# Two ordering keys in a hand-planned attention and MLP kernel: the ranks of the flags behind a far-V product, the far V of tile 3 behind a mask of tile 2

## The chip, the cores and the metric

The kernel runs on one core of a Trainium2 chip. The metric is the device time of one execution in microseconds (us); lower is better. A core has five engines that run their own instruction streams in order and meet at semaphores: TensorE (PE, matmuls), VectorE (DVE), ScalarE (ACT), GpSimd (POOL) and SyncE (SP, which here only issues DMAs). In the profile PEld is the loading of TensorE's weights.

## What is computed

Attention over 4 batches, 8 heads, 768 positions and head size 64, followed by a two-layer MLP over the 3072 tokens that come out of it:

```python
scores = scale * np.matmul(q, k.transpose(0, 1, 3, 2))
stream_keep = causal & (is_sink | in_win)          # 4 sink positions, a window of 64
mask = np.where(retr, causal, stream_keep)         # one flag for each head: full or streaming
a = softmax(np.where(mask, scores, -1e9)); attn_out = np.matmul(a, v)
x = attn_out.transpose(0, 2, 1, 3).reshape(B * S, H * D)
h = x @ w_in                                        # 512 -> 2048
g = h - np.tanh(h)
return g @ w_out                                    # 2048 -> 512
```

The flags (`is_retrieval`) are data: the kernel learns only on the chip which heads are full and which are streaming. Inputs and output are float32; the kernel's matmuls are float16.

## The kernel before, in words

**Tiles.** The 3072 tokens are 12 tiles of 256 (`TT`), three tiles to a batch (`NG`), so tiles 0 to 2 are batch 0 and tiles 3 to 5 batch 1. A tile has four pairs of heads; pair number n is 4 t + hp, so tile 2 has pairs 8 to 11. For each pair the kernel transposes q and k (`st_T`, or DMA transposes, `turn`), multiplies them (`st_S`, PE L1063, with the exponential on ACT at L1076), masks the block at the diagonal on DVE (`mask`: L1117 in tile 2, L1127 and L1092 from tile 3 on), multiplies by V (`st_A`, PE L1156) and divides by the sums (DVE L1176, L1188 or L1203). Tiles 0 and 1 have their mask added by a matmul (L1052) instead.

**The MLP of a tile.** `H_unit` makes 256 columns of the hidden layer: eight matmuls (PE L1267) into a PSUM bank, a tanh on ACT (`th`, L1279), and one DVE instruction `gt` (L1286) that reads the bank and the tanh, forms h - tanh(h) and lets the bank go. `O_group` multiplies by `w_out` (PE L1325); ACT copies the result out (`ot`, L1299) and SP stores it (L1311).

**Far V.** For a key block that lies before the window, a streaming head may see the sinks alone. So the kernel keeps V twice: `v1` as it is, and `vf`, the far V, where the rows that a streaming head must not see are zero. In batch 0 GpSimd makes `vf` by `scale_v` (L725), one product for each of the key blocks 0 to 3: blocks 0 and 1 come with tile 0, blocks 2 and 3 with tile 1. From batch 1 on, heads are sorted by their flag, and `vf` is made by `spread` (L690 products, L699 and L710 copies, all on GpSimd).

**Ranks of the flags.** `by_rank` (L834) sorts the heads: 15 small DVE instructions (L841 to L908), four mask builders `m4r` (L917) and two copies for `mS`; then GpSimd and DVE each read the ranks into registers (L939). `gather` for tile 3 and later (GpSimd L636 and L672) picks heads by these registers out of the raw loads (`rawqk`, `rawv`, L592). Tile 3's raw loads are issued from GpSimd's queue, behind the register read for all but the first of them; those of later tiles from SP.

**Tile 4's gate.** A small GpSimd instruction pair `hold` (L576, L580) writes into tile 4's raw buffers once the last part of `w_out` has landed; so SP can't issue the loads of tile 4 before it.

**What sets the order.** All work is first listed by `Plan.op(engine, estimated ns, function, r=keys read, w=keys written)`. An entry depends on the last writer of each key that it reads. `Plan.run` then plays the list through with its estimates: whenever an engine comes free, it takes, of the entries whose dependencies are done, the one with the lowest number (number in the list, unless `prio` is given). It also hands out the PSUM banks and models that a DVE entry with `port=True` waits for a GpSimd entry that holds the port. What comes out is one fixed order for each engine; the functions are then called in that order. A key is known to the planner alone. The waits that the chip obeys come from the tiles that instructions really share, so a key that names data which an instruction doesn't touch moves the instruction in its engine's order and adds no wait on the chip.

**The two places.** `LATE` is a list of keys that each of the 15 small instructions of `by_rank` reads besides its own; before, it is `("x16", 3)`, which is written by the DVE instruction that divides the last pair of tile 0. `spread(3)` lists two L690 products, the L699 copy and the L710 copy; before, they read only `v1` and the flags.

Of the kernel before, what the change touches and what calls it, by code (L numbers as in the profile page):

```python
# [16 lines left out]
class Plan:  # L17
# [28 lines left out]
    def op(self, eng, ns, fn, r=(), w=(), dma=None, prio=None, port=False):  # L46
        i = len(self.ops)
        deps = set()
        for k in r:
            if k in self.writer:  # L50
                deps.add(self.writer[k])
            if k[0] in self.PSUM:
                deps.update(j for j in self.readers.get(k, ()) if self.ops[j][0] != eng)
            self.readers.setdefault(k, []).append(i)
        for k in w:
            if k in self.writer:
                deps.add(self.writer[k])
            elif k[0] in self.BANKS:
                self.first[i] = self.first.get(i, ()) + (k,)
            deps.update(self.readers.get(k, ()))  # L60
            self.writer[k] = i
            self.readers[k] = []
        for key in (*r, *w):
            if isinstance(key, tuple) and key[0] in self.BANKS:
                self.held.setdefault(key, set()).add(i)
            elif isinstance(key, tuple) and key[0] in self.bufs:
                self.users.setdefault(key[:2], []).append(i)
        deps.discard(i)
        self.ops.append((eng, ns, fn, deps, dma, i if prio is None else prio, port))
        return i  # L70
# [185 lines left out]
def kernel(  # L256
# [17 lines left out]
    HP = H // 2  # L274
# [5 lines left out]
    NG = S // TT  # L280
# [6 lines left out]
    fast = n_sink_i <= 64 and window_i <= 64  # L287
# [3 lines left out]
    def pool(name, bufs=1, **kw):  # L291
# [30 lines left out]
    rflagr = const.tile([128, NGEN], FP32, name="rflagr")  # L322
    rflagr0 = const.tile([128, NGEN], FP32, name="rflagr0")
    thrr = const.tile([128, NGEN], FP32, name="thrr")
    mS = const.tile([128, 5, 128], FP16, name="mS")
# [13 lines left out]
        pt=([128, 2, 512 * NG], FP16), ptn=([128, 2, 512], FP16),  # L339
        x16=([128, NB, 2, D], FP16), x16t=([128, NB, H, D], FP16), rinv=([128, NB, 2], FP32),  # L340
# [13 lines left out]
    GATE = {3: (1, 0), 4: (1, 1)}  # L354
    CUT1 = (-10.5,-6.0,2.25,13.5)
    FLEX = 2
    LEAD = 3
    QUART = 7
    LD = 22
    GA = 8  # L360
    FROM = 3
    BR = 1
    FRONT = "A40"
    LATE = [("x16", 3)]
    BEHIND = [("x16", 1)]
    MASKS = 2
    A2 = (4, 9)
# [2 lines left out]
    def program(first):  # L370
# [43 lines left out]
        def dma(ring, ns, fn, packets, each, r=(), w=(), paced=False, lag=(1100, 1500)):  # L414
            r = list(r) + [FRONT] * (ring == "POOL")
            op(ring, ns, fn, r=r, w=w, dma=(packets, each, paced) + lag)
# [265 lines left out]
        def spread(t):  # L682

            b, g = divmod(t, NG)
            lo = g * NB
            for jb in range(lo, min(lo + NB, 4)):
                fl = rflagr0 if jb == 0 else rflagr
                op(
                    "POOL", 600,
                    lambda jb=jb, fl=fl: nc.gpsimd.tensor_mul(  # L690
                        out=vfs[b]()[:, jb, 0:NGEN, :], in0=v1s[b]()[:, jb, 0:NGEN, :],
                        in1=fl[:].unsqueeze(2).to_broadcast([128, NGEN, D + 1]),
                    ),
                    r=[("v1", b, jb, 0), "rflagr0", "rflagr"], w=[("vf", b, jb, 0)],
                )
            if g == 0:
                op(
                    "POOL", 1060,
                    lambda: nc.gpsimd.tensor_copy(  # L699
                        out=vfs[b]()[0:64, :, NGEN:H, :],  # L700
                        in_=v1s[b]()[0:64, 0, NGEN:H, :].unsqueeze(1).to_broadcast(
                            [64, 4, H - NGEN, D + 1]
                        ),
                    ),
                    r=[("v1", b, 0, 1)], w=[("vf", b, "low")],
                )
            j0, j1 = max(lo, 1), min(lo + NB, 5)
            op(
                "POOL", 60 + 260 * (j1 - j0),
                lambda: nc.gpsimd.tensor_copy(  # L710
                    out=vfs[b]()[64:128, j0 - 1 : j1 - 1, NGEN:H, :],
                    in_=v1s[b]()[64:128, j0:j1, NGEN:H, :],
                ),
                r=[("v1", b, jb, 1) for jb in range(j0, j1)],
                w=[("vf", b, "up", jb) for jb in range(j0, j1)],
            )

# [116 lines left out]
        def by_rank():  # L834

            def dve(ns, fn, r, w):
                op("DVE", ns, fn, r=r + LATE, w=w, port=True)

# [75 lines left out]
            for h in range(NGEN):  # L914
# [6 lines left out]
                    r=["thrr", "A4", "A40", "A41", "A43"], w=["m4r"], port=True,  # L921
# [7 lines left out]
                r=["A4", "A40", "A41", "A43"], w=["mS"], port=True,  # L929
# [1 line left out]
            op(  # L931
                "DVE", 180,
                lambda: nc.vector.tensor_copy(out=mS[:, 4, :], in_=mS[:, 2, :]),
                r=["mS3"], w=["mS"], port=True,
            )
            for e, et in (("POOL", Engine.Pool), ("DVE", Engine.DVE)):

# [64 lines left out]
        pts = {}  # L1002

        def is_near(n):
            return ranked(n // HP) and n % 2
# [336 lines left out]
        def visits(t):  # L1342
            g = t % NG
            gen = [t * HP + hp for hp in range(HP) if not is_near(t * HP + hp)]
            near = [t * HP + hp for hp in range(HP) if is_near(t * HP + hp)]
            if near:
                a, c = gen
                d, e = near
                return {
                    0: [[(a, 0), (d, 0)], [(c, 0), (e, 0)]],  # L1350
                    1: [[(a, 0), (a, 1)], [(d, 0), (c, 0)], [(c, 1), (e, 0)]],
                    2: [[(a, 0), (a, 1)], [(a, 2), (d, 0)], [(c, 0), (c, 1)], [(c, 2), (e, 0)]],
                }[g]
            if g == 0:
                return [[(n, 0)] for n in gen]
            units = [(n, gi) for n in gen for gi in range(g + 1)]
            return [units[i : i + 2] for i in range(0, len(units), 2)]
# [96 lines left out]
        def att_pairs(t):  # L1454

            seq = []
            g = t % NG
            for hp in range(HP):
                n = t * HP + hp
                seq.append(lambda n=n: st_T(n, TE))  # L1460
                units = [(n, gi) for gi in range(g + 1)]
                for i in range(0, len(units), 2):
                    seq.append(lambda u=units[i : i + 2]: st_S(u))
                if hp:
                    seq += [lambda n=n - 1, j=j: st_A(n, j) for j in range(NB)]
                    if not by_dma(t):
                        seq.append(lambda n=n - 1: st_X(n))
            n = t * HP + HP - 1
            seq += [lambda n=n, j=j: st_A(n, j) for j in range(NB)]
            if by_dma(t):  # L1470
                seq.append(lambda: st_X_tile(t))
            else:
                seq.append(lambda n=n: st_X(n))
            return seq
# [32 lines left out]
        def spread_over(fs, lo, hi):  # L1507
            for i, f in enumerate(fs):
                plan.setdefault(max(0, int(lo + (hi - lo) * i / max(len(fs), 1))), []).append(f)

        if first and fast:
            spread_over([by_rank], BR, BR)
        spread_over(att_pairs(1) + [lambda: scale_v(1, SV)], 0, 0)
# [3 lines left out]
        def point(h):  # L1517
            t, ts = divmod(h, 2)
            return slot_of[t, 4 * ts + 3] if t >= 2 else max(0, 13 + 2 * h)

        for b in range(FLEX, NTT // NG) if first and fast else ():
            left = {}
# [4 lines left out]
            for i, vis in enumerate(vs):  # L1527
                s = point(6 * b - LEAD + i)
                for t in sorted({n // HP for n, gi in vis}):
# [10 lines left out]
                for t in range(b * NG, b * NG + NG):  # L1540
                    if max(left[n] for n in range(t * HP, t * HP + HP)) == i:
                        fs.append(lambda t=t: st_X_tile(t))
        for t in range(NG, FLEX * NG if first and fast else NTT):
            b, g = divmod(t, NG)
# [11 lines left out]
                spread_over(attention(t), lo, hi)  # L1556

        for s, what in enumerate(slots):
            if first and fast and s == point(2 * NG * FLEX - LEAD - 1):
                P.split = len(P.ops)  # L1560
            fs = plan.get(s, [])
            mid = (len(fs) + 1) // 2
            for i, x in enumerate(what):
                for f in fs[:mid] if i == 0 else ():
                    f()
                if x[0] == "H":
                    H_unit(*x[1:])
                else:
                    t, ts, f0, f1, c0, c1 = x[1:]
                    O_group(t, ts, f0, f1, c0, c1)  # L1570
                for f in fs[mid:] + between.get(s, []) if i == 0 else ():
                    f()
# [59 lines left out]
```

## Time and profile before

| | |
|---|---|
| runs, us | 231.21, 232.74, 232.95 |
| median, us | 232.74 |
| the profiled execution: its own time, us | 233.06 |
| its span (first to last instruction), us | 231.3 |
| mean granted TensorE clock | 0.990 |
| PE busy in the span, us | 221.7 (96%) |
| DVE / ACT / POOL busy, us | 146.7 / 139.9 / 97.5 |

The profiled execution is 0.32 us above the median of the runs shown, and its own time is 1.76 us more than its span. In the views a row of the timeline reads: start, duration, engine, line, operation, output <- input, shape, count, and in brackets the idle time of that engine before it and what ended it. A row with x2 stands for two instructions and the time from the start of the first to the end of the last. A queue's engine (SPq, POOLq) is the sequencer that issues.

### The profile page before, as it was taken

The page shows a single profiled execution, that of the slowest core. Times are in us where ns is not written, and L with a number is a line of the kernel's source. Part 1 is how long each engine was busy: PE and PEld are TensorE (multiplying, and loading weights), DVE is VectorE, ACT ScalarE, POOL GpSimd, SP SyncE. Part 2 cuts the span into 40 slices and gives each one's busy share as a digit, 9 for nine tenths or more (in the row PEclk, how much of TensorE's full clock was granted, in tenths as well). Part 3 has the DMA queues.
Part 4 walks back from the last instruction along what each step waited for, and adds up shares of the span by engine and source line. Part 5 has one row for each costly group of instructions (what it writes and reads, how often), then busy time and mean ns, then how long its engine had stood idle before and what let it go on. Part 6 is the DMA issues. An engine that isn't in the chain of part 4 may idle for free.

```text
span 231.3 us, 6135 instructions
## 1 busy us (share of the span) xinstructions
PE 221.7 (96%) x2328; PEld 158.7 (69%) x2328; DVE 146.7 (63%) x355; ACT 139.9 (60%) x214; POOL 97.5 (42%) x231
## 2 busy tenths in 40 slices
PE   7879999989999999999999999999999999999992
PEld 6446788768887666766776676765957767766652
DVE  5878887893774766755774776466867547534400
ACT  3817837975566858747547756846875867534420
POOL 8998361980281918684363968280000000000000
PEclk9988999999999999999999999999999999999999
DMA  6999999979999999999979999944121211220112
GB/s 171 150 194 206 186 223 217 208 114 204 198 202 233 195 197 233 206 198 209 248 149 252 222 250 185 212 117 114 48 45 48 60 34 45 67 47 28 48 63 80
DMA packets 102964, 35.31 MB, mean 153 GB/s; under 512 B 90642, under 2 KB 100114, under 8 KB 102930
## 3 DMA queue, kind: packets, MB, share of 16 engines
q1 hardware_dynamic: 85632, 27.14, 56.3%
q0 software_dynamic: 17152, 7.60, 25.1%
q8 instruction: 19, 0.31, 0.6%
q14 instruction: 15, 0.12, 0.2%
q10 hardware_dynamic: 146, 0.13, 0.2%
HBM read 27.26 MB, written 6.29 MB: 145 GB/s over the span
## 4 chain that ended last, share of the span: by engine, by line
PE 84%; DVE 6%; DMA 3%; POOL 2%; ACT 2%; issue 1%; POOLq 0%; DVEq 0%
PE banks L1325 36%; PE banks L1267 34%; PE banks L1063 7%; PE banks L1156 6%; DMA t16p<-in_k_dram 3%; DVE gt L1286 2%; DVE pt L1117 2%; ACT pt L1076 1%; DVE prod L846 1%; POOL v L490 1%; PE banks L968 1%; PE banks L1052 1%; ACT th L1279 1%; DVE QK L951 0%; POOL A L736 0%
## 5 line engine op out<-in xcount | busy, mean ns | idle before, releaser
L1267 PE MATMUL banks<-xT,win 128*128 128x256 f16 x768 | 95.0, 273 | 0.7 <-DVE gt L1286 0.5
L1325 PE MATMUL banks<-wout,gt 128*128 128x512 f16 (+1 forms) x464 | 94.5, 343 | 1.1 <-DVE gt L1286 1.1
L1286 DVE SCALAR_TENSOR_TENSOR gt<-th,banks 128x512 f16<-128x512 f32 x96 | 65.1, 682 | 31.5 <-ACT th L1279 30.7
L1267 PEld LDWEIGHTS <-win 128*128 128x128 f16 x768 | 72.8, 98 | 15.5 <-issue 2.1
L1279 ACT ACTIVATE th<-banks 128x512 f32<-128x512 f32 x96 | 57.1, 601 | 40.5 <-PE banks L1267 39.4
L1076 ACT ACTIVATE pt<-banks 128x768 f16<-128x768 f32 (+1 forms) x60 | 52.9, 920 | 17.3 <-PE banks L1063 16.4
L1325 PEld LDWEIGHTS <-gt 128*128 128x128 f16 x464 | 43.0, 98 | 29.3 <-DVE gt L1286 1.3
L636 POOL CAST t<-rawqk 128x256 f16 x72 | 28.6, 443 | 30.6 <-DMA rawqk<-in_k_dram 14.7
L1299 ACT ACTIVATE ot<-banks 128x512 f32<-128x512 f32 (+1 forms) x28 | 15.0, 535 | 22.0 <-PE banks L1325 21.2
L1188 DVE TENSOR_TENSOR x16t<-banks,rinv 128x128 f32 (+1 forms) x80 | 22.9, 288 | 1.8 <-DVE x16t L1188 0.2
L1099 DVE TENSOR_TENSOR ptn<-ptn,mS 128x512 f16<-128x512 f16 x24 | 10.9, 493 | 17.0 <-ACT ptn L1076 17.0
L1063 PE MATMUL banks<-QK 64*128 64x128 f16 (+1 forms) x364 | 21.4, 241 | 0.0
L672 POOL CAST v<-rawv 128x128 f16 x72 | 19.7, 320 | 0.0
L1063 PEld LDWEIGHTS <-QK 64*128 64x128 f16 x364 | 12.7, 95 | 9.9 <-issue 6.8
L1076 ACT ACTIVATE ptn<-banks 128x1024 f16<-128x1024 f32 (+1 forms) x18 | 17.2, 953 | 3.8 <-PE banks L1063 3.7
L1156 PEld LDWEIGHTS <-pt 128*128 128x128 f16 x420 | 16.3, 97 | 3.8 <-ACT pt L1076 0.7
L1156 PE MATMUL banks<-v,pt 128*128 128x65 f16 x220 | 16.6, 193 | 0.3 <-ACT pt L1076 0.2
L1127 DVE TENSOR_TENSOR pt<-pt,m4r 128x1024 f16<-128x1024 f16 (+1 forms) x18 | 12.4, 686 | 5.0 <-ACT pt L1076 5.0
L1176 DVE RECIPROCAL rinv<-banks 128x4 f32<-128x4 f32 x48 | 8.5, 177 | 8.5 <-PE banks L1156 7.7
L1156 PE MATMUL banks<-vf,pt 128*128 128x65 f16 x200 | 13.1, 193 | 0.0
L661 POOL COPY kc<-QK 128x128 f16<-128x128 f16 x12 | 3.5, 290 | 12.0 <-DMA QK<-t 11.9
L1156 PEld LDWEIGHTS <-ptn 128*128 128x128 f16 x132 | 6.4, 97 | 2.2
(79 smaller groups left out, 137.2 us busy)
## 6 DMA issues: line engine op xcount, KB each, us to landing
out_dram<-ot SPq DMA_DIRECT2D x19, 256.0 KB, 2.5
rawqk<-in_q_dram SPq DMA_DIRECT2D x18, 256.0 KB, 3.8
rawqk<-in_k_dram SPq DMA_DIRECT2D x18, 256.0 KB, 4.4
rawv<-in_v_dram SPq DMA_DIRECT2D x16, 256.0 KB, 4.6
win<-in_moe_w_in_dram POOLq DMA_DIRECT2D x4, 512.0 KB, 11.3
wout<-in_moe_w_out_dram POOLq DMA_DIRECT2D x4, 512.0 KB, 13.2
out_dram<-ot SPq DMA_DIRECT2D x9, 128.0 KB, 3.8
v<-in_v_dram POOLq DMA_DIRECT2D x6, 128.0 KB, 6.8
```

Of the source, the lines that this page charges most:

```text
L636: nc.gpsimd.tensor_copy(out=c5()[:, :, :, s_ : s_ + 1, :], in_=r5()[:, :, :, at, :])
L672: nc.gpsimd.tensor_copy(out=v1s[b]()[:, g * NB : g * NB + NB, RANK[s_] : RANK[s_] + 1, 0:D], in_=rv()[:, :, at, :],)
L1063: nc.tensor.matmul(out=sc()[:, hh, o : o + nb * 128], lhsT=lhsT, rhs=QK[p_, hp, q_0 : q_0 + nb * 128], start=not added, stop=not added or ...
L1076: lambda pt=pt, sc=sc, gi=gi, wid=wid: nc.scalar.activation(out=pt()[:, :, 512 * gi : 512 * gi + wid], in_=sc()[:, :, 0:wid], func=AF.Exp, ...
L1127: nc.vector.tensor_mul(out=pv, in0=pv, in1=m)
L1156: nc.tensor.matmul(out=av()[:, i, hh, :], lhsT=pt()[:, hh, co : co + 128], rhs=vv, start=(jb == first_jb), stop=(jb == qb),)
L1188: nc.vector.tensor_mul(out=xt()[:, :, at, :], in0=av()[:, :, hh : hh + 1, 0:D], in1=rinv()[:, :, hh : hh + 1].unsqueeze(3).to_broadcast([1 ...
L1267: nc.tensor.matmul(out=ph()[:, j, :], lhsT=w_in_t[fb // 4][:, cb, f0 : f0 + 128], rhs=xT()[:, :, cb, :], start=(cb == 0), stop=(cb == HP - 1),
L1279: lambda: nc.scalar.activation(out=th()[:], in_=ph()[:], func=AF.Tanh, scale=1.0 / XS),
L1286: lambda: nc.vector.scalar_tensor_tensor(out=gt()[:, u * FU : (u + 1) * FU, :], in0=th()[:], scalar=-XS, in1=ph()[:], op0=ALU.mult, op1=AL ...
L1299: nc.scalar.activation(out=ot()[:, c0:c1], in_=po()[:, c0:c1], func=AF.Copy, scale=1.0 / XS)
L1325: nc.tensor.matmul(out=po()[:, c0:c1], lhsT=gt()[:, f, ts * 128 : ts * 128 + 128], rhs=w_out_t[:, f, c0:c1], start=(f == 0), stop=(f == NF ...
```

## The change

It adds some parameters that are off (`TRI = ()`, `SPLIT = 1 << 30`, `MSL = []`; with these values the code that reads them does what it did before) and turns two keys:

```diff
-    LATE = [("x16", 3)]
+    LATE = [("vf",0,3,0)]
+    AFTER = {3: 2}
+    TRI = ()
+    SPLIT = 1 << 30
+    MSL = []
...
         def spread(t):
             b, g = divmod(t, NG)
             lo = g * NB
+            after = [("pt", pts[AFTER[t] * HP + HP - 1][1], 0)] if t in AFTER else []
...
-                    r=[("v1", b, jb, 0), "rflagr0", "rflagr"], w=[("vf", b, jb, 0)],
+                    r=[("v1", b, jb, 0), "rflagr0", "rflagr"] + after, w=[("vf", b, jb, 0)],
...
-                    r=[("v1", b, 0, 1)], w=[("vf", b, "low")],
+                    r=[("v1", b, 0, 1)] + after, w=[("vf", b, "low")],
...
-                r=[("v1", b, jb, 1) for jb in range(j0, j1)],
+                r=[("v1", b, jb, 1) for jb in range(j0, j1)] + after,
...
-                r=["mS3"], w=["mS"], port=True,
+                r=["mS3"] + MSL, w=["mS"], port=True,
...
-            if first and fast and s == point(2 * NG * FLEX - LEAD - 1):
+            if first and fast and s == min(SPLIT, point(2 * NG * FLEX - LEAD - 1)):
```

`("vf", 0, 3, 0)` is the far V of key block 3 in batch 0: it is written by the last of the four L725 products on GpSimd. `("pt", pts[11][1], 0)` is the exponential of pair 11, the last of tile 2, first group; its last writer in the list is that pair's mask (L1117). So in the planner the small instructions of `by_rank` may not start before the fourth product is done, and the four instructions of `spread(3)` not before the last mask of tile 2 is done. `visits` gets a branch for tiles in `TRI`, which is empty.

More of the change, by code (lines that the diff above doesn't have):

```diff
@@ L1348, in visits @@
                 d, e = near
+                if t in TRI:
+                    return {
+                        0: [[(a, 0), (d, 0), (c, 0)], [(e, 0)]],
+                        1: [[(a, 0), (a, 1), (d, 0)], [(c, 0), (c, 1), (e, 0)]],
+                        2: [[(a, 0), (a, 1), (a, 2)], [(d, 0), (c, 0), (c, 1)], [(c, 2), (e, 0)]],
+                    }[g]
                 return {
```

## The prediction

> **What bounds the kernel now.** I read the table of stages first (busy time of each engine in windows of the span), to see where PE, the engine with 96% of the span, is not busy; columns are the window, its length, then PE, PEld, DVE, ACT and POOL busy.
>
> ```profile
> 20.00:25.00 5.00, 4.46 (x59) 3.00 (x58) 4.97 (x21) 3.62 (x6) 2.85 (x4) 1.00 1.31 202
> ...
> 50.00:55.00 5.00, 4.02 (x56) 3.33 (x57) 2.90 (x8) 3.08 (x5) 1.07 (x4) 1.00 0.85 171
> ...
> 65.00:100.00 35.00, 35.00 (x389) 25.17 (x387) 23.90 (x55) 24.95 (x37) 20.61 (x56) 1.00 1.12 207
> 100.00:150.00 50.00, 50.00 (x500) 34.55 (x498) 30.97 (x69) 31.57 (x48) 30.10 (x83) 1.00 1.05 215
> ```
>
> From 65 to 150 us PE has no idle time. So whatever PE gains ahead of that is passed on, and nothing can be gained there. Ahead of it two holes stand out: 0.54 us in the window from 20 and 0.98 us in the window from 50. Then the chain of work that ended last, for what ends those holes (start, duration, what):
>
> ```profile
> 18.80 2.39 DVE prod L846
> ...
> 21.21 0.22 DVE cnt L851
> 21.43 0.60 DVE gt L1286
> ...
> 22.08 1.47 PE banks L1267 x12
> ...
> 36.10 0.22 PE banks L1325 x2
> ...
> 47.41 2.71 DVE pt L1117 x2
> ...
> 50.33 0.60 DVE gt L1286
> ...
> 50.98 0.83 PE banks L1325 x6
> ```
>
> Both times the path goes through DVE: PE waits for a `gt`, and the `gt` stands in DVE's queue behind one slow instruction: `prod` of the ranks (2.39 us for 64 columns) and a pair of masks of tile 2 (2.71 us). The timelines of DVE and of GpSimd tell why they are slow:
>
> ```profile
> 18.69 2.49 DVE L846 TENSOR_TENSOR prod<-upto,rflag 128x64 f32<-128x64 f32 x1
> ...
> 21.35 0.68 DVE L1286 SCALAR_TENSOR_TENSOR gt<-th,banks 128x512 f16<-128x512 f32 x1
> ...
> 23.31 0.21 DVE L875 TENSOR_TENSOR prod<-pos_b,iota 128x64 f32<-128x64 f32 x1
> 23.45 0.68 DVE L1286 SCALAR_TENSOR_TENSOR gt<-th,banks 128x512 f16<-128x512 f32 x1
> ...
> 36.26 1.29 DVE L1117 SCALAR_TENSOR_TENSOR pt<-m,pt 128x512 f16<-128x512 f16 x2 [0.23 <-ACT pt L1076]
> ...
> 47.33 2.80 DVE L1117 SCALAR_TENSOR_TENSOR pt<-m,pt 128x512 f16<-128x512 f16 x2
> ...
> 50.84 1.38 DVE L1117 SCALAR_TENSOR_TENSOR pt<-m,pt 128x512 f16<-128x512 f16 x2
> 52.51 0.18 DVE L1176 RECIPROCAL rinv<-banks 128x4 f32<-128x4 f32 x1 [0.28 <-PE banks L1156]
> ```
>
> ```profile
> 19.02 2.07 POOL L725 TENSOR_TENSOR vf<-v,rflag 128x520 f16<-128x520 f16 x2
> ...
> 35.62 0.88 POOL L614 DMA_DIRECT2D wout<-in_moe_w_out_dram  x1 [1.70 <-DMA wout<-in_moe_w_out_dram]
> ...
> 46.58 1.19 POOL L690 TENSOR_TENSOR vf<-v,rflagr 128x260 f16<-128x260 f16 x2
> 47.73 1.04 POOL L699 COPY vf<-v 64x1040 f16<-64x1040 f16 x1
> 48.83 0.76 POOL L710 COPY vf<-v 64x260 f16<-64x260 f16 x1
> 49.65 0.53 POOL L576 CAST rawqk<-wout 1x4 f32<-1x4 f16 x1
> ...
> 50.79 0.28 POOL L661 COPY kc<-QK 128x128 f16<-128x128 f16 x1
> 56.20 0.31 POOL L432 MEMSET v<- 128x48 f16 x1 [5.13 <-PE banks L1156]
> 62.11 2.81 POOL L636 CAST t<-rawqk 128x256 f16 x8 [5.60 <-DMA out_dram<-ot]
> ```
>
> A `prod` of the same size takes 0.21 us at 23.31, where GpSimd runs nothing; the one at 18.69 ends (21.18) just after GpSimd's two far-V products (21.09). A pair of masks takes 1.29 us at 36.26 with GpSimd idle, and 2.80 us at 47.33 beside `spread(3)`, which ends at 49.59. The `gt` at 21.35 takes the same 0.68 us as the one at 23.45: it is not slowed itself, it only stands behind.
>
> **Ranks behind the last far-V product.** Nothing is added or removed; the 15 small instructions move later in DVE's order, and since they touch no `vf`, no wait comes with it. What now stands ahead of them is every DVE entry that is ready before the fourth product's end at 21.09. Two tanhs are ready by then:
>
> ```profile
> 19.25 0.60 ACT L1279 ACTIVATE th<-banks 128x512 f32<-128x512 f32 x1 [0.30 <-PE banks L1267]
> 20.12 0.60 ACT L1279 ACTIVATE th<-banks 128x512 f32<-128x512 f32 x1 [0.28 <-PE banks L1267]
> ...
> 48.76 1.94 ACT L1076 ACTIVATE pt<-banks 128x1024 f16<-128x1024 f32 x2 [0.57 <-PE banks L1063]
> ```
>
> Their `gt`s can run from 19.85 and 20.72 on, instead of at 21.35 and 23.45. PE's hole ahead of 22.08 is 0.54 us (4.46 of 5.00 busy) and closes: the first `gt` would end at about 20.55, before the hole begins at 21.54. The ranks then start at about 21.4, after the products, and their `prod` should cost some 0.2 us: saved DVE time 2.49 - 0.21 = 2.28 us, of which only the 0.54 us lies on the path. Is the gain kept? The nearest limit is the landing of a `w_out` part: GpSimd's issue at 35.62 waited for it, and the chain has PE's `w_out` products at 36.10. If that is the part that they read, PE can gain no more than 36.10 - 35.62 = 0.48 us there. Bounds 0 and 0.54; I take 0.5, nearest to both rows. `cnt` was done at 21.43 before, and will be at about 21.8, with two `gt`s fewer (2 x 0.6 us) behind it; so the ranks come no later, nor do GpSimd's register read and the loads of tile 3 behind it.
>
> **Far V of tile 3 behind the last mask of tile 2.** Again an order alone, now on GpSimd. Behind the four instructions (1.19 + 1.04 + 0.76 = 2.99 us) stood, in this order, the `hold` pair, the `kc` copies up to 50.79, the memset at 56.20 and `gather(4)` at 62.11. The first two groups now go ahead of them: the `hold`, and with it SP's first loads of tile 4, by up to 49.65 - 46.58 = 3.07 us. `kc` can't go before its DMA transposes have landed, and those are not shown to be later than 50.79; so I put the moved block at about 50.8 to 53.8. The memset and `gather(4)` have 5.13 and 5.60 us of waiting ahead of them, which covers it; without that cover tile 4 would be late by up to 2.99 us. The products' results are first read by tile 4.
>
> Gain: the mask pair at 47.33 falls back towards 1.29 us, 1.51 less than 2.80. The `gt` behind it moves from 50.25 to about 48.8, and PE's stop ahead of 50.98 goes: the PE rows below put that stop at 1.06 us (from 49.92), so the change is worth that there and no more. What is late next: the last mask of tile 2. It waits for the second of the two exponentials at 48.76 (end 50.70, with the first part's gain about 50.2), so it runs at 50.2 to 51.5 and its second half meets the moved block. PE has room for that, as its rows at 53.11 and 55.30 show:
>
> ```profile
> 22.08 1.47 PE L1267 MATMUL banks<-xT,win 128*128 128x256 f16 x12 [0.54 <-DVE gt L1286]
> ...
> 50.98 0.83 PE L1325 MATMUL banks<-wout,gt 128*128 128x256 f16 x6 [1.06 <-DVE gt L1286]
> ...
> 53.11 2.36 PE L1325 MATMUL banks<-wout,gt 128*128 128x256 f16 x20
> 55.30 0.25 PE L1156 MATMUL banks<-vf,pt 128*128 128x65 f16 x3
> ```
>
> The product with V of pair 11 at 55.30 waits for this mask, which was done at 52.22: 3.1 us of room, 1.5 us of it used up if PE is earlier by as much. A mask late by up to 1.5 us therefore costs PE nothing there. But the division of pair 10 (52.51) stands behind the mask on DVE and keeps a PSUM bank. Bounds for this part 0 and 1.06; I take 0.9, near the upper one, since the rows before 50.98 show one stop and the rows after it a lot of `w_out` work.
>
> The row at 47.33 has a pair of masks losing 1.51 us to three kinds of GpSimd instruction. The Trainium skill, SBUF — State Buffer, section Who interferes with whom, says that the port which DVE and GpSimd share is a lock held for one whole instruction, by the one that issues first, while the other blocks. By that rule the moved block takes the port once between the halves of the last mask, nothing of the 1.06 us is given back, and the sum would be 1.56 us, 231.2 us by the median. The trace agrees that one blocks the other, and not with the order: the `prod` that began at 18.69 gave way to two products that began at 19.02.
>
> **Sum.** 0.5 + 0.9 = 1.4 us. The profiled execution's 233.06 would be 231.66; by the median of the runs shown, which lies 0.32 below it, 232.74 - 1.4 = 231.3 us, 0.6% faster. About 1% is what a measurement of this kernel can tell from no change.
>
> **The rivals.**
> - Half of it: one of the two holes is filled by another wait, such as the `w_out` landing at 35.6 or the bank of pair 10. For it: both limits lie within a microsecond of the path. Against it: each touches one part alone. 232.74 - 0.7 = 232.0 us.
> - The change doesn't do what it says: since the keys add no wait on the chip, the moved block may still run beside the masks, if GpSimd, freed from it at 46.58, gets through `hold` and `kc` early. `hold` and `kc` would also meet the mask at 47.33. For it: only the upper end of the transposes' landing is shown. Against it: SP's other transposes and `kc` at 50.79 follow the same order. 232.7 us.
> - Slower: the moved block holds DVE up at the last mask from 50.2 on for its whole 2.99 us. The mask would end at 50.2 + 1.29 + 2.99 = 54.5, and the division of pair 10 behind it, which ran at 52.51 before, would run 2.0 us later than before. If its bank is the next that PE needs, all that follows is late by as much: 232.74 + 2.0 = 234.7 us. It decides once the block holds the mask for over 1.0 us (2.99 - 2.0), from where on the division is later than before. For it: the row at 47.33. Against it: there the pair lost 1.51 us to the same block, half of 2.99, and PE has 2.36 us of `w_out` work that needs no new division.
> - Larger: the reordering also takes out stops that are hidden in rows of busy PE, by another 1 us: 230.3 us. Against it: of all that PE waited for between 15 and 62 us, the view of waits (total, times, longest) has 1.6 us in the two holes and 0.4 us beside them:
>
> ```profile
> PE banks L1325 <- DVE gt L1286: 1.1, 1, 1.1
> PE banks L1267 <- DVE gt L1286: 0.5, 1, 0.5
> PE banks L1238 <- DVE x L1203: 0.4, 1, 0.4
> ```
>
> **How the numbers follow.** Forecast 0.55, half of it 0.15, nothing 0.10, slower 0.10, larger 0.10. The three runs spread from 231.21 to 232.95, 0.75%, so the forecast's own 231.3 can measure from 229.8 (231.21 - 1.4) up; the half and nothing cases reach 233, the slower one 234.7. Low end 229.8, high end 233.7: left out are most of the slower case and a part of the larger. Faster by over 1% (below 230.4): the larger case and about a fifth of the forecast's, 0.20. Slower by over 1% (above 235.1): the slower case where it also delays tile 3, which its 234.7 does not hold, 0.08. Within 1%: 0.72.
>
> **What would show it right or wrong.** Right: the first `prod` at about 0.2 us and behind two `gt`s; the PE stop ahead of the third `H_unit` gone; the mask pair of pair 10 near 1.3 us; L690 of tile 3 behind the `kc` copies, from about 50.8; SP's first load of tile 4 before 50.20; PE's window from 50 near 5.00 busy; the end earlier by the sum of the two holes. Wrong: a `prod` of over 1 us still beside L725; a PE stop at 35.6 for `w_out`; the last mask of tile 2 over 2 us with PE idle behind it; or any PE idle time after 62 us, which would mean that a load, not PE, sets the pace there.

## The result, and the profile after

| | runs | median, us | range, us | ratio to before, 95% interval |
|---|---|---|---|---|
| before | 17 | 232.66 | 231.21 to 233.51 | |
| changed | 17 | 231.17 | 230.20 to 232.07 | 0.9942 [0.9923, 0.9961] |

The changed kernel is 0.6% faster: 232.66 x 0.0058 = 1.35 us, between 0.9 and 1.8 us. Its profiled execution took 231.54 us with a span of 229.8 us, 1.5 us less than the span of before. From the first line of the diff on, line numbers are larger by 4 or 5: the ranks' `prod` is L851, the mask L1122, `gt` L1291, the `spread` products and copies L695, L704 and L715.

Where the time went is read best between the same matmuls in both traces: the stretches begin at the scores of the second pair of tile 1, then of tile 2, of tile 2's last pairs, of tile 3 and of tile 4. Stretches of before (window, length, busy time of PE, PEld, DVE, ACT and POOL, granted clock):

```profile
20.63:34.56 13.93, 13.27 (x169) 10.44 (x168) 12.21 (x42) 8.63 (x13) 7.50 (x9) 1.00 1.58 205
34.56:48.33 13.77, 13.63 (x178) 11.03 (x178) 11.32 (x23) 11.75 (x18) 8.22 (x20) 1.00 1.19 201
48.33:56.07 7.74, 6.68 (x99) 5.41 (x99) 4.57 (x9) 4.32 (x6) 2.62 (x6) 1.00 0.78 159
56.07:73.38 17.31, 17.31 (x183) 14.65 (x182) 11.78 (x28) 10.04 (x18) 7.38 (x22) 1.00 1.08 205
```

The same stretches of the changed kernel:

```profile
21.12:34.42 13.30, 13.14 (x171) 10.50 (x170) 11.65 (x42) 8.58 (x13) 7.12 (x9) 1.00 1.60 204
34.42:48.03 13.61, 13.61 (x177) 11.04 (x176) 11.19 (x24) 11.71 (x18) 6.53 (x17) 1.00 1.25 197
48.03:54.54 6.51, 6.51 (x99) 5.50 (x98) 3.38 (x8) 4.22 (x6) 4.71 (x8) 1.00 0.94 211
54.54:71.85 17.31, 17.31 (x183) 14.66 (x181) 11.79 (x28) 10.05 (x18) 7.42 (x22) 1.00 1.04 207
```

The stretch of the ranks is shorter by 0.63 us, the one of tile 2's masks by 1.23, the one between them by 0.16, and the one from tile 3 to tile 4 by nothing, since PE is busy in all of it. Up to the first of these matmuls the changed kernel *lost* 0.49 us (21.12 against 20.63). Sum: 0.63 + 0.16 + 1.23 - 0.49 = 1.53 us, which is the span's 1.5.

DVE in the changed kernel, at the three places:

```profile
13.65 1.50 DVE L938 COPY mS<-mS 128x128 f16<-128x128 f16 x1
...
20.37 0.69 DVE L1291 SCALAR_TENSOR_TENSOR gt<-th,banks 128x512 f16<-128x512 f32 x1 [0.73 <-ACT th L1284]
21.24 0.69 DVE L1291 SCALAR_TENSOR_TENSOR gt<-th,banks 128x512 f16<-128x512 f32 x1 [0.18 <-ACT th L1284]
...
22.17 0.19 DVE L851 TENSOR_TENSOR prod<-upto,rflag 128x64 f32<-128x64 f32 x1
...
47.04 1.28 DVE L1122 SCALAR_TENSOR_TENSOR pt<-m,pt 128x512 f16<-128x512 f16 x2
...
48.44 0.68 DVE L1291 SCALAR_TENSOR_TENSOR gt<-th,banks 128x512 f16<-128x512 f32 x1
50.44 1.72 DVE L1122 SCALAR_TENSOR_TENSOR pt<-m,pt 128x512 f16<-128x512 f16 x2 [1.32 <-ACT pt L1081]
```

`prod` takes 0.19 us where it took 2.49, and stands behind both `gt`s. The mask pair of pair 10 takes 1.28 us where it took 2.80. The last mask meets the moved block and takes 1.72 us. (In a second profile of this kernel `prod` began at 20.72, before the far-V products ended at 21.12, and took 0.50 us; it stood behind both `gt`s there too.) GpSimd in the changed kernel:

```profile
14.24 0.88 POOL L527 DMA_DIRECT2D t16p<-in_q_dram  x1
...
48.59 0.18 POOL L580 CAST rawqk<-wout 1x4 f32<-1x4 f16 x1 [2.24 <-ACT th L1284]
...
50.24 0.29 POOL L665 COPY kc<-QK 128x128 f16<-128x128 f16 x1
50.50 2.13 POOL L695 TENSOR_TENSOR vf<-v,rflagr 128x260 f16<-128x260 f16 x2
52.58 1.04 POOL L704 COPY vf<-v 64x1040 f16<-64x1040 f16 x1
```

The moved block runs from 50.50, behind the last `kc`; the gate (`hold`, L580) at 48.59 instead of 49.65. The view of waits, of PE alone between 15 and 62 us, shows that in this profile no `gt` stops PE any more (total, times, longest):

```profile
PE banks L1243 <- DVE QK L956: 1.2, 1, 1.2
PE banks L1272 <- DVE xT L956: 0.2, 1, 0.2
```

The first row is the loss at the start: DVE's `mS` copy took 1.50 us, and the DVE work queued behind it held PE up until 15.23.

### The profile page after: what moved, and what is told of

The parts are those of the page before. It is cut to its first block, busy times and chain, and to the rows that moved or that the text cites. A ratio compares the mean times of both kernels' runs of the same rounds, so it can differ in the third digit from the quotient of the medians.

```text
span 229.8 us, 6134 instructions
## 1 busy us (share of the span) xinstructions
PE 221.1 (96%) x2328; PEld 158.8 (69%) x2328; DVE 144.8 (63%) x355; ACT 139.6 (61%) x214; POOL 98.3 (43%) x231
## 4 chain that ended last, share of the span: by engine, by line
PE 91%; DMA 3%; POOL 2%; DVE 1%; issue 1%; ACT 0%; POOLq 0%; DVEq 0%
PE banks L1272 37%; PE banks L1330 37%; PE banks L1068 8%; PE banks L1161 7%; DMA t16p<-in_k_dram 3%; PE banks L1057 1%; POOL v L494 1%; PE banks L973 1%; DVE mS L938 1%; POOL A L741 0%; POOL t16p L527 0%; PE banks L1243 0%; DVE xT L956 0%; DVE x L1208 0%; ACT ot L1304 0%
## 5 line engine op out<-in xcount | busy, mean ns | idle before, releaser
L1291 DVE SCALAR_TENSOR_TENSOR gt<-th,banks 128x512 f16<-128x512 f32 x96 | 65.1, 683 | 32.0 <-ACT th L1284 31.2
L1181 DVE RECIPROCAL rinv<-banks 128x4 f32<-128x4 f32 x48 | 9.4, 197 | 7.0 <-PE banks L1161 6.4
L695 POOL TENSOR_TENSOR vf<-v,rflagr 128x260 f16<-128x260 f16 x12 | 8.6, 743 | 0.0
```

The costliest lines, as they stand in the source:

```text
L1291: lambda: nc.vector.scalar_tensor_tensor(out=gt()[:, u * FU : (u + 1) * FU, :], in0=th()[:], scalar=-XS, in1=ph()[:], op0=ALU.mult, op1=AL ...
```

## The experiments

The theory: a DVE instruction with two operands in SBUF (`prod`, the masks) and a GpSimd instruction that reads SBUF block one another; the change takes both pairs apart, and DVE's time is what it gains. The first rival: the order itself, or an earlier gate of tile 4, gives the gain, and the contention is a side show. Each kernel is the changed one with the edit shown (`...` stands for lines left out); PE's, ACT's and SP's instruction orders are the same in all of them, but for ten added matmuls in the two with the longer fill. Where entries were moved by hand, the planner's finished order was edited just before it is emitted:

```diff
-    def run(self):
+    def run(self, moves=()):
...
+        for i, j in moves:
+            order.remove(i)
+            order.insert(order.index(j) + 1, i)
```

The first four kernels ran on one chip, the next four on a second and the last four on a third, each time with the kernel before beside them. So the ratios can be compared, and medians only within such a group.

| kernel | median, us | ratio to before on the same chip, 95% interval |
|---|---|---|
| ranks alone | 232.32 | 0.9986 [0.9959, 1.0013] |
| far V alone | 231.17 | 0.9946 [0.9919, 0.9973] |
| far V twice | 232.31 | 1.0002 [0.9968, 1.0035] |
| writes at the old place | 230.78 | 0.9941 [0.9908, 0.9975] |
| `prod` back | 231.24 | 0.9961 [0.9947, 0.9975] |
| gate late, loads ahead of it | 231.04 | 0.9947 [0.9933, 0.9961] |
| `mS` copy late | 231.12 | 0.9957 [0.9944, 0.9971] |
| longer fill | 231.19 | 0.9958 [0.9945, 0.9971] |
| the changed kernel again | 230.94 | 0.9953 [0.9930, 0.9975] |
| gate and loads late | 234.41 | 1.0098 [1.0067, 1.0129] |
| gate first, far V old | 230.98 | 0.9941 [0.9918, 0.9963] |
| `mS` late and longer fill | 230.93 | 0.9940 [0.9920, 0.9960] |

**Each half alone.** First the ranks' key without the far V's:

```diff
-    AFTER = {3: 2}
+    AFTER = {}
```

> The changed kernel with the far V of tile 3 back at its old place, so only the ranks are moved; on PE, ACT and SP the order is that of both kernels. Theory (a blocked prod holds up a gt): the first prod near 0.2 us, two gt ahead of it, the mask pair at 47 still near 2.8 us with a PE stop of about 1 us behind it; time 0.4 to 0.5 us under the kernel before, ratio 0.998 to 0.9985. Rival (the hole at 22 us is filled by another wait, as the landing of w_out at 35.6): prod is short all the same, but PE is no earlier at 36 us, ratio 0.9995 to 1.0005.

It gains 0.3 us, between -0.3 and 0.95: not told from nothing. (None of its 12 runs has a mean granted clock below 0.995; 10 of the 35 of before have. The part on the start of the ranks says why that matters.) Its profile has more to say. DVE, then GpSimd, then PE:

```profile
46.02 1.88 DVE L1122 SCALAR_TENSOR_TENSOR pt<-m,pt 128x512 f16<-128x512 f16 x2
```

```profile
46.30 2.08 POOL L695 TENSOR_TENSOR vf<-v,rflagr 128x260 f16<-128x260 f16 x2
...
50.44 0.53 POOL L580 CAST rawqk<-wout 1x4 f32<-1x4 f16 x1
```

```profile
53.85 0.51 PE L1068 MATMUL banks<-QK 64*128 64x256 f16 x10
...
72.23 0.56 PE L1068 MATMUL banks<-QK 64*128 64x256 f16 x10 [0.59 <-DMA QK<-t]
```

Here the mask came first and GpSimd's two products were held up most: 2.08 us instead of 1.19. The mask pair lost about 0.4 us (1.88 against the 1.46 of kernels that have no block here). PE has no 1-us stop at the masks. But the gate stands behind the block on GpSimd and comes at 50.44, so what SP issues behind it is late, tile 4's loads above all, and from tile 3's scores to tile 4's PE needs 72.23 - 53.85 = 18.38 us instead of 17.31. The time lost is the same, 1.07 us, on another path.

Then the far V's key without the ranks':

```diff
-    LATE = [("vf",0,3,0)]
+    LATE = [("x16", 3)]
```

> The changed kernel with the ranks back at their old place, so only the far V of tile 3 is moved behind the last mask of tile 2. Theory (masks blocked by GpSimd): mask pair of pair 10 near 1.3 us, no PE stop near 50 us, the first prod still near 2.4 us with the stop of 0.5 us behind it; 0.9 to 1.06 us under before, ratio 0.9955 to 0.9962. If the two parts only work together, the ratio is over 0.998.

It gains 1.25 us, between 0.6 and 1.9: nearly all of the change. DVE in it:

```profile
17.75 0.60 DVE L851 TENSOR_TENSOR prod<-upto,rflag 128x64 f32<-128x64 f32 x1
...
19.73 0.69 DVE L1291 SCALAR_TENSOR_TENSOR gt<-th,banks 128x512 f16<-128x512 f32 x1 [1.12 <-ACT th L1284]
```

With the ranks at the old place `prod` was through at 18.35 this time, before the two products began (19.21), and the `gt` was in time. Its 0.60 us are a shorter meeting, with the third product, which ended at 18.25. So the hole that the forecast saw is not there in every execution. PE waited for something else instead, a part of `w_in`:

```profile
18.01 1.92 PE L1272 MATMUL banks<-xT,win 128*128 128x256 f16 x16 [1.14 <-DMA win<-in_moe_w_in_dram]
```

**Contention or order.** Far V of tile 3 stays moved, and the same four instructions run once more at the old place, into a spare tile that nothing reads:

```diff
...
+            if t == 3:
+                twice(b)
...
+        def twice(b):
+            for jb, fl in ((0, rflagr0), (1, rflagr)):
...
+                        out=spare[:, 0 : NGEN * (D + 1)].rearrange("p (h d) -> p h d", h=NGEN),
...
```

> The changed kernel, with four more GpSimd instructions that do the far V of tile 3 a second time into a spare tile at the old place, beside the masks of tile 2 (the result is not used); the order of all other work is that of the changed kernel, and the gate of tile 4 stands behind them as before. Theory: the mask pair at 47 goes back to 2.5 to 2.9 us, PE stops again about 1 us near 50, and the gain of the far V is lost: ratio 0.998 to 1.000. Rival (the last mask, next to the real far V, is the one that counts): ratio stays near 0.994.

The whole gain is gone. GpSimd and DVE:

```profile
47.00 2.08 POOL L730 TENSOR_TENSOR spare<-v,rflagr 128x260 f16<-128x260 f16 x2
...
51.14 0.53 POOL L581 CAST rawqk<-wout 1x4 f32<-1x4 f16 x1
```

```profile
46.72 1.88 DVE L1155 SCALAR_TENSOR_TENSOR pt<-m,pt 128x512 f16<-128x512 f16 x2
```

Again the mask began first and GpSimd lost most; the gate came at 51.14, and tile 4's scores were late by 0.57 us. By 113 us it had lost 1.1 us to the changed kernel's first profile, with a second wait for transposed Q and K on the way (0.37 us ahead of 84.30). Some 0.4 us more went after that, in a stretch that was not followed up.

In the next kernel the spare tile is filled at the old place by four memsets, which read nothing:

```diff
+        def fill(b):
+            for ns in (600, 601, 1060, 320):
+                op(
+                    "POOL", ns, lambda n=ns: nc.gpsimd.memset(spare[:, 0 : min(1040, n)], 0.0),
...
```

> The same as the doubled far V, but with four memsets of a spare tile in its place: GpSimd is busy and only writes, and the gate of tile 4 again stands behind them. If the masks are slowed by what GpSimd reads (the second SBUF input of a mask comes through the shared read port), the mask pair stays near 1.3 us and the ratio near 0.994, although the gate comes later. If any GpSimd work slows them, the pair is over 2 us and the ratio 0.998 to 1.000. If the gain comes from the earlier loads of tile 4 behind the gate, the ratio is 0.998 to 1.000 with a short mask pair.

```profile
44.53 1.96 POOL L677 CAST v<-rawv 128x128 f16 x8
46.43 2.70 POOL L729 MEMSET spare<- 128x600 f16 x4
49.09 0.18 POOL L581 CAST rawqk<-wout 1x4 f32<-1x4 f16 x1
```

```profile
46.18 1.46 DVE L1132 SCALAR_TENSOR_TENSOR pt<-m,pt 128x512 f16<-128x512 f16 x2
```

2.70 us of GpSimd work beside the mask pair, nearly as long as the block (2.99), cost it nothing: in the kernel with the far V alone, where GpSimd runs nothing after the casts at this place, the pair takes 1.46 us as well. What it has over 1.28 is the end of the casts (L677, up to 46.49), which read SBUF: wherever the pair takes 1.46 us it begins 0.3 us before the casts end, and wherever it takes 1.28 it begins after them. So it is not that GpSimd is busy, but that it reads, and the first rival falls as far as the masks go. The gate at 49.09 was early enough, and the gain is whole.

**The gate.** The two cases in which GpSimd lost make the gate a suspect of its own. The first try only moved the gate (entry 295 of the list) behind the moved block:

```diff
-            P.run()
+            P.run([(295, 344)] if first else ())
```

> The changed kernel with the gate of tile 4 put behind the moved far V on GpSimd, so that SP's loads of tile 4 start at about 53.9 instead of 48.8, later than the 50.2 of before; masks and ranks stay as changed. Theory that the masks alone carry the gain: ratio stays near 0.994. Rival that the gate is a second path (a late gate makes tile 4's QK late, as in the runs with the far V alone at its old place and doubled): PE waits for the QK transposes ahead of the first scores of tile 4, by the 5.1 us less the 1.4 us that QK lands ahead and less what SP makes up, 1 to 3 us; ratio 0.998 to 1.006.

It tested nothing: the edit also put the gate behind SP's first loads in the order of emission, so these no longer waited for it, and in this kernel the gate overwrites a few values of tile 4's raw inputs. The second try moves the first three loads along, and the two stores that follow them in SP's order:

```diff
-            P.run()
+            P.run([(295, 344), (296, 295), (297, 296), (298, 297), (434, 298), (453, 434)] if first else ())
```

> The changed kernel with the gate of tile 4 behind the moved far V on GpSimd, and with SP's first three loads of tile 4 and the two stores after them kept behind the gate, so that they start at about 54.3 instead of 48.8 (in the run e10 the loads had come ahead of the gate and were not late). Masks and ranks stay as changed. Theory that the masks alone carry the gain: ratio 0.994 to 0.996. Theory that the gate is a second path beside the masks: tile 4's QK lands 2 us or more later, past the 1.4 us that it has, PE waits for QK ahead of tile 4's scores as in e1 and e4, ratio 0.998 to 1.004.

```profile
53.82 0.18 POOL L583 CAST rawqk<-wout 1x4 f32<-1x4 f16 x1
```

```profile
53.97 0.51 PE L1071 MATMUL banks<-QK 64*128 64x256 f16 x10
...
73.85 0.56 PE L1071 MATMUL banks<-QK 64*128 64x256 f16 x10 [0.49 <-DMA QK<-t]
```

The masks are undisturbed (1.46 and 1.39 us), and the kernel is 3.47 us slower than the changed one beside it (230.94), slower than before too. From tile 3 to tile 4 it takes 19.88 us, 2.57 more than PE needs. So a late gate costs by itself. It does so through all that SP issues behind it, and not through tile 4's loads alone: on the way PE waited 0.68 us for a bank that ACT copied out late (the copy had waited for a store), 1.00 us for `xT` (its transpose was issued at 58.01 instead of 55.38) and 0.49 us for tile 4's Q and K. In the kernel with the ranks alone it was 0.24 us for `xT` and 0.59 us for Q and K. Across the profiles, the gate's start ahead of tile 3's first scores, and how late tile 4's scores then are:

| kernel | gate | scores of tile 3 | room, us | scores of tile 4 late by, us |
|---|---|---|---|---|
| before | 49.65 | 56.07 | 6.42 | 0 |
| changed | 48.59 | 54.54 | 5.95 | 0 |
| writes at the old place | 49.09 | 53.69 | 4.60 | 0 |
| ranks alone | 50.44 | 53.85 | 3.41 | 1.07 |
| far V twice | 51.14 | 54.55 | 3.41 | 0.57 |
| gate and loads late | 53.82 | 53.97 | 0.15 | 2.57 |

In these profiles the room that is needed lies between 3.4 and 4.6 us. Then the other way round: no key for the far V at all, and the gate moved ahead of its block.

```diff
-    AFTER = {3: 2}
+    AFTER = {}
...
-            P.run()
+            P.run([(295, 336)] if first else ())
```

> The kernel with the ranks alone moved, the far V of tile 3 without the new key, and the gate of tile 4 put ahead of the far V in GpSimd's order: the far V waits behind the gate for the last part of w_out and runs at about 48 to 51, after the mask pair of pair 10 and beside the last mask. Theory (a pair of masks slowed beside the far V, or a gate behind it, each costs about 1 us; the last mask has room): most of the gain is there without the new key, ratio 0.994 to 0.996. Rival (the far V has to be clear of the last mask too): mask pair of pair 11 over 2 us, PE stops, ratio 0.997 to 1.000.

```profile
47.97 0.18 POOL L583 CAST rawqk<-wout 1x4 f32<-1x4 f16 x1 [1.36 <-ACT th L1287]
...
48.24 1.19 POOL L698 TENSOR_TENSOR vf<-v,rflagr 128x260 f16<-128x260 f16 x2
```

```profile
46.63 1.28 DVE L1125 SCALAR_TENSOR_TENSOR pt<-m,pt 128x512 f16<-128x512 f16 x2
...
50.04 1.74 DVE L1125 SCALAR_TENSOR_TENSOR pt<-m,pt 128x512 f16<-128x512 f16 x2 [1.33 <-ACT pt L1084]
```

The gate waits for `w_out` (by the kernel's text: its row names ACT), and this wait keeps the block behind it away from the first mask pair, which ended at 47.91. The gain is as large as the change's. It doesn't part the two causes, but shows that one move in one queue serves both.

**The start of the ranks.** `prod` alone back to its old place, the other fourteen where the change has them:

```diff
-            P.run()
+            P.run([(196, 177)] if first else ())
```

> The changed kernel with one DVE instruction, the first prod of the ranks, put back to where it stood before (behind the last QK copy of tile 1, ahead of both gt); nothing else is moved. Theory (a prod that meets the far-V products of GpSimd holds up the gt): where the QK copies end at about 18.8, prod takes about 2.4 us and PE stops about 0.5 us ahead of the third H unit; where they end a microsecond earlier, prod gets through in about 0.6 us and nothing is lost; ratio to before 0.994 to 0.9965. Rival (it is the whole block of ranks ahead of the second gt that costs): ratio as the changed kernel, 0.994, whatever prod takes.

```profile
17.59 1.11 DVE L854 TENSOR_TENSOR prod<-upto,rflag 128x64 f32<-128x64 f32 x1
...
18.95 0.69 DVE L1294 SCALAR_TENSOR_TENSOR gt<-th,banks 128x512 f16<-128x512 f32 x1 [0.24 <-ACT th L1287]
```

It ended at 18.70, ahead of the two products (from 19.19 in this profile), and no `gt` stopped PE. This is not the case that the forecast was made for. What goes with the difference is PE's granted clock. The window from 15 to 20 us of before, of this kernel, and of the longer fill (below):

```profile
15.00:20.00 5.00, 5.00 (x41) 3.32 (x42) 4.05 (x11) 2.32 (x3) 4.96 (x6) 0.66 1.24 207
```

```profile
15.00:20.00 5.00, 4.60 (x56) 3.19 (x56) 4.57 (x12) 2.92 (x4) 4.94 (x6) 1.00 1.24 204
```

```profile
15.00:20.00 5.00, 4.10 (x46) 2.90 (x46) 3.27 (x10) 2.63 (x4) 4.96 (x6) 1.00 1.24 206
```

At 0.66 PE is slower by a third at this place. In the six profiles with 0.66 tile 1's Q and K copies end between 18.3 and 19.6, in before at 18.80, and there `prod` behind them meets the products; in the eight with 1.00 they end between 17.2 and 17.9. That `prod` is slow at the low clock is seen in one profile only, before's; no other kernel with `prod` at the old place was profiled in that condition. At 1.00 the next limit shows: in seven of the eight profiles PE then waited for the landing of a part of `w_out` (0.2 us at about 35 us), and in six for a part of `w_in` (0.4 to 1.5 us, up to 17.2 to 18.0 us). Two edits went for the start. One puts the `mS` copy behind the last `m4r`:

```diff
-            P.run()
+            P.run([(215, 213)] if first else ())
```

> The changed kernel with one DVE copy (mS, L938) moved from ahead of tile 1's QK copies to behind the last mask builder of the ranks, where GpSimd is idle. In the changed kernel's profile it took 1.50 us, until GpSimd's DMA issue ended, and PE stopped 1.2 us there; in five other profiles it took 0.58 us. Theory: a matter of chance in each run, so the median gains 0.1 to 0.4 us and the slowest runs most; ratio to before 0.992 to 0.994. Rival: the copy just waits for the same port later and the next stage's DMA issues; ratio 0.994 to 0.996.

One makes the fill matmuls (at 11.85, 128 columns each, their result unread), which give PE work ahead of this place, fifteen instead of five:

```diff
+        for i, k in more.items():
+            self.size[i] += k
...
+            P.run({115: 10} if first else {})
```

> The changed kernel with ten more 128-column matmuls in the fill that PE runs at 11.85, whose result nobody reads, in front of 0.9 us in which PE waits. In three of six profiles PE's granted clock is 0.50 from about 15.5 to 18.5, in the other three 1.00. Theory (the clock drops where PE was idle for half of 12 to 15 us): the clock stays 1.00, and the median falls by half of the 0.8 us that lies between these profiles: ratio 0.991 to 0.993, with the runs closer together. Rival (with the clock full PE waits for w_in there, 0.6 to 1.1 us in two profiles): ratio 0.993 to 0.995.

And both together:

```diff
-            P.run()
+            P.run(*([(215, 213)], {115: 10}) if first else ())
```

> The changed kernel with both the mS copy late and the longer fill, as a version that might beat it: each alone was no faster on another chip than the changed kernel. Theory (both take away losses of some runs only, and what PE gains ahead of 40 us it gives back at the mask of pair 9 beside the gather of tile 3): ratio equal to that of the changed kernel in this call within 0.002. Rival: 0.002 to 0.004 below it.

The fill held the clock at 1.00 in both profiles. None of the three is faster than the changed kernel: 230.93 with both edits, beside 230.94 without any on the same chip. With the longer fill tile 2's scores began at 33.56 us, 0.9 earlier than in the changed kernel's first profile (34.42); by tile 3's (54.20 against 54.54) most of it was gone. In the changed kernel's second profile, at clock 1.00 without the fill, they began at 33.03 and 53.45. The changed kernel once more:

> The changed kernel itself, beside the other kernels of this call on the same chip. It should give 0.994 to 0.9955 as before; in its profile the mS copy should take 0.58 us as in most runs, and the scores of tile 3 start near 54.

Its clock was 1.00 and its `mS` copy 0.58 us, and its span 228.7 us; no kernel here beats it by more than its interval.

## Why the prediction was right, point by point

- **What bounds the kernel: right.** All that PE gained by tile 3's scores (1.53 us) was there at tile 4's and in the span (1.5 us), and no PE wait shows between 62 and 100 us.
- **Ranks, 0.5 us: right in the forecast's profile, too large as a mean.** The stretch got shorter by 0.63 us. But of the two profiles with all ranks at the old place only the one with clock 0.66 has the hole, and the edit alone measured 0.3 us, with an interval that holds nothing as well as 0.6. What the ranks' half is worth in the mean stays open. The bound that was put on it by the landing of `w_out` (0.48 us) did not hold it in the first profile, where PE shows no such wait; in the second, where PE is further ahead, PE waits 0.24 us for `w_out`. `cnt` ended at 22.84 instead of the forecast's 21.8, 1.4 us later than before, and this cost nothing: the last raw load of tile 3 was issued at 31.37 instead of 31.98.
- **Far V, 0.9 us: right in kind, too small.** The stretch of the masks got shorter by 1.23 us (1.06 of stop, and 0.17 less busy time of the same 99 matmul records), and alone it measured 1.25 us, between 0.6 and 1.9. The upper bound of 1.06 was the stop in one trace.
- **"The `hold`, and with it SP's first loads of tile 4", named without a price: the step that was incomplete.** The forecast counted the earlier gate as free. It is a second path to the same loss: if the mask starts first, GpSimd loses, the gate is late, and PE comes to tile 4's scores 0.6 to 1.1 us late instead of waiting 1.06 us for a `gt`. The changed kernel shuts both paths. By the kernels with the ranks alone and with the far V twice, little is gained where the mask goes first and the gate stays behind a held block. The gate came 1.06 us earlier (48.59 against 49.65), not the 3.07 that were the forecast's limit: it now waits for `w_out`.
- **Last mask beside the moved block: right.** 1.72 us, and PE passes it without a stop. So the rival "slower", in which DVE is held for the whole block, fell: the mask pair lost under 0.5 us (1.72 against 1.28). "Half of it" and "doesn't do what it says" fell by the rows above.
- **Not foreseen: the start.** 0.49 us were lost at 13.65, in one execution, not by the change: its second profile doesn't show it. That the profiled spans differ by nearly the sum of the forecast, 1.5 against 1.4, is partly luck: 0.13 us more than forecast from the ranks, 0.33 more from the masks and 0.16 between them are set off by 0.49 lost at the start.
- **Who gives way.** The prediction held the order of starts against the rule of the Trainium skill, SBUF — State Buffer, section Who interferes with whom (the one that issues first holds the shared port, the other blocks). At the masks the runs bear the rule out as to who gives way. Before, L690 began at 46.58 and the mask at 47.33, and the mask lost; in two experiments the mask began first (46.02 and 46.72, against 46.30 and 47.00) and GpSimd lost most. They do not bear out that the wait lasts for one instruction: the mask pair of before lost 1.52 us, while only 0.44 us were left of the second product (to 47.77), and the copy behind the products took from 47.73 the same 1.04 us as without a mask beside it. The Trainium skill says in the same section that a DVE instruction with two inputs in SBUF meets only GpSimd instructions that read SBUF, and the memsets agree (1.46 us with and without them). It stays open why the `prod` of 18.69 (behind copies that ended at 18.80) gave way to products that began at 19.02. The DMA issue that GpSimd ran just ahead of them is not enough for it: with `prod` back alone, `prod` ended at 18.70 in the middle of that issue.

```profile
18.23 0.94 POOL L497 DMA_DIRECT2D v<-in_v_dram  x1
```

## What to carry to other kernels

Where two engines block one another, the loser changes with their starts by a few tenths of a microsecond, so price both: what waits behind the slow DVE instruction, and what waits behind the slow GpSimd one. A bound taken from the stop that one trace shows is the price of one of the two outcomes only. The cheapest way out may be to put an instruction that has to wait anyway ahead of the one that disturbs, in the same queue.

## What the runs showed of the hardware

- **A held `prod` ends with GpSimd's product.** In seven profiles the first `prod` met far-V products, and in six of them it ended 0.09 or 0.10 us after one: 21.18 after 21.09 in before, 21.22 after 21.12 in the changed kernel's second profile, 18.35 after 18.25 with the far V alone. The exception is `prod` back (18.70 after 18.29), where a DMA issue ran behind the product.

- **A DMA issue on GpSimd holds up a DVE copy from SBUF to SBUF.** The `mS` copy starts at 13.65 and 13.66 in the two profiles of the changed kernel, inside a GpSimd issue that ends about 14.25. In the second it ends with that issue, at 14.24. In the first it missed the gap and ended at 15.15, with the next issue (14.24 + 0.88 = 15.12). Put late, it met another issue and ended with it too (26.20 + 0.61 = 26.81, the issue at 25.93 + 0.89 = 26.82); with the gate first it ran where one issue ended (13.24) and the next had not begun (13.53), from 13.15 to 13.31, and took 0.16 us. The second profile:

```profile
13.66 0.58 DVE L938 COPY mS<-mS 128x128 f16<-128x128 f16 x1
```

- **The granted clock falls at one place in some executions, whatever the kernel.** Without the longer fill, 6 of 12 profiles have 0.66 in the window from 15 to 20 us, the others 1.00; their mean clock is 0.993 or less and 0.997 or more. By that mark (below 0.995) it fell in 28 of 113 runs of these versions, before left aside, and in none of the 17 of them with the longer fill. In the 5 us ahead PE is busy for 3.17 to 3.49 us in the six profiles where it fell, for 3.43 to 3.96 in the six where it did not, and for 4.00 and 4.04 with the longer fill; so the busy share does not settle it near 3.45. This fits the Trainium skill, TensorE: Matmul & The Clock Gate, section Part 1, by which PE's activity gates its clock, in a window that runs free of the kernel, so that the same kernel can come out differently. What a low clock costs is not settled: on the third chip the changed kernel's median was 231.73 us in 4 runs with it and 230.62 in 8 without; the kernel before had 232.25 in 7 and 232.47 in 21 there, and 232.95 in 10 and 232.70 in 25 on the first chip. So the runs of before do not show that its hole behind `prod`, which was profiled at the low clock, costs them time.
